# Transposing the activation rows of later chunks: a DRAM regroup plus VectorE transposes in place of DMA transposes, in a parallel attention and gated-MLP block

## The chip, the cores and the metric

The kernel runs on one core of one Trainium2 chip. The metric is the device time of one execution in microseconds (us). Three executions of the kernel before took 308.99, 309.40 and 310.95 us; their median, 309.4 us, is the time before. The profile comes from one more execution, of which the hardware recorded a span of 307.5 us from its first to its last instruction.

## What is computed

One layer whose attention and MLP branches read the same normalised rows and are added to the input. Shapes: x is 2048 rows by 640, 32 heads of 20, a sliding window of 256 keys, MLP width 1536, all in bfloat16.

```python
def reference(A_x, A_wqkv, A_wo, B_x, B_w_gate, B_w_up, B_w_down):
    xn = _layernorm(x)                               # over the 640 features
    q, k, v = split_heads(xn @ A_wqkv)               # 32 heads of 20
    s = (q @ k.T) * 20 ** -0.5                       # kept where 0 <= i - j < 256
    attn = (softmax(where(mask, s, -1e9)) @ v) @ A_wo
    mlp = (sigmoid(xn @ B_w_gate) * (xn @ B_w_up)) @ B_w_down
    return x + attn + mlp
```

Every matrix product with `xn` contracts over the 640 features, so TensorE needs the rows turned: features on the partitions, rows along the free dimension. How the rows of a chunk get turned is what the change is about.

## The kernel before

The 2048 rows are cut into four chunks of 512 rows (`c` = 0 to 3), each in four blocks of 128 rows (`s`). For each chunk there is one buffer `xnT[c]`, 128 partitions by 5 by 512: five slices `d`, each holding 128 of the 640 features for the 512 rows. Gate and up (`g_gu`, L407 to L423), the q and k projections (`proj_block`, L292) and v (`project_v`, L323) read it slice by slice and accumulate over the five slices.

**Input rows.** `xc[c]` holds the raw rows of a chunk. Its pool `xp` has a single buffer, so the load of the next chunk (`load_x`, L137) waits until every reader of the one before is done. Chunk 0 comes in four blocks over SyncE's queue (SP): L162 to L166, the first being all 128 rows of block 0.

**Chunk 0** is normalised block by block by VectorE (DVE) and ScalarE (ACT), and turned by TensorE (PE) against an identity matrix (`transpose_rows`, L276), five transposes a block.

**Chunks 1 to 3** are normalised by `g_norms` (L343): statistics per block, a pause of a few steps, then four times `norm_block` (L270, a DVE instruction that writes `xn`). Each `xn` is then turned by a DMA transpose on SP's queue, `turn_block` (L282): four per chunk, for chunk 3 in a generator of its own, `g_turns` (L361).

**Order.** Nothing is scheduled by a planner: the instructions of each engine stand in the order in which the code issues them. The attention runs over steps `t` (16 for chunk 0, 20 for each later one). A step issues a group of score matmuls into the single PSUM tile `ps` (L487), an exponential on ACT (L493) and two mask selects on GpSimd (L504) or a minimum on DVE (L497). Between steps, a list of filler parts (`Fill`) is pulled, each a generator that yields the PE time of what it has just issued. `mix(a, b, ...)` weaves a generator `b` into the steps of `a`. The parts around the change stand in this order (L689 to L707):

- `gu0a`, `gu0b`: gate and up of chunk 0, with the 11 or so steps of `norms1` woven in
- `x2`: the load of chunk 2's rows (L140), then `wo_i` (eight DRAM-to-DRAM DMAs, L212), `wd` (five DMAs, L205), `pads` (two DMAs that clear scratch, L178)
- `qk1`: the ten projection blocks of chunk 1. Each fills one of four PSUM tiles of `ps_d`; DVE (q, L301) or ACT (k, L303) copies it to `st`, a ring of six SBUF tiles (L118); SP stores `st` to a DRAM scratch (L305), from where `spread` (L315) brings heads back as `qT` and `kT`. After the fourth q block, `load_wo` (L217) issues four DMAs
- `v1`, `out0` (the down and output projections of chunk 0, with `norms2` woven in), `x3`, `qk2`, and so on

The same four PSUM tiles of `ps_d` serve the q, k, v, gate, up, down and output matmuls and the accumulators of the attention output (`acc`, L520). All SP work, loads, stores and transposes, stands in one queue and is issued in order; by the semaphores of the built program, each DMA also waits until the one eight places before it has landed.

`make_edge` (L238) fills a constant mask tile once: one memset and four selects, all on GpSimd, issued after the projections of chunk 0.

The weights are loaded with feature `c * 128 + p` on partition `p` of slice `c`:

```python
    wqkv_r = A_wqkv.rearrange("(c p) n -> p c n", p=P)
```

Of the kernel before, what the change touches and what calls it, by code (L numbers as in the profile page):

```python
# [9 lines left out]
P = 128  # L10
S = 2048
D = 640
# [3 lines left out]
DC = D // P  # L16
FC = F // P
CW = 512
NCH = S // CW
SBC = CW // P  # L20
# [6 lines left out]
FS = 768  # L27
# [9 lines left out]
BIG = 3.0e38  # L37
BF16 = mybir.dt.bfloat16
# [7 lines left out]
U = 64  # L46
# [47 lines left out]
def kernel(  # L94
# [11 lines left out]
    nc = tc.nc  # L106
    x2 = A_x.flatten_outer_dims()
    out2 = out.flatten_outer_dims()
    xr = x2.rearrange("(n p) d -> p n d", p=P)
# [25 lines left out]
    xc = {}  # L135

    def load_x(c):  # L137
        t = xp.tile([P, SBC, D], BF16, name="xc")
        xc[c] = t
        nc.sync.dma_start(out=t, in_=xr[:, c * SBC:(c + 1) * SBC, :])  # L140

    wqkv = [const.tile([P, DC, D], BF16, name="w" + part) for part in "qkv"]
    wqkv_r = A_wqkv.rearrange("(c p) n -> p c n", p=P)
    wg = [const.tile([P, DC, FS], BF16, name=f"wg{k}") for k in range(F // FS)]
    wu = [const.tile([P, DC, FS], BF16, name=f"wu{k}") for k in range(F // FS)]
    wd = const.tile([P, FC, D], BF16, name="wd")
# [5 lines left out]

    xc[0] = xp.tile([P, SBC, D], BF16, name="xc")

    def load_rows(s, queue):
        queue.dma_start(out=xc[0][:, s, :], in_=xr[:, s, :])  # L156

    def load_v(hf):
        a = hf * HALF
        nc.sync.dma_start(out=wqkv[2][:, :, a:a + HALF], in_=wqkv_r[:, :, 2 * D + a:2 * D + a + HALF])  # L160

    load_rows(0, nc.sync)  # L162
    load_rows(1, nc.sync)
    load_rows(3, nc.sync)
    load_v(0)
# [13 lines left out]

    def load_gu(t, w, k, lo=0, hi=FS):  # L180
        nc.sync.dma_start(out=t[k][:, :, lo:hi],
                          in_=w.rearrange("(c p) f -> p c f", p=P)[:, :, k * FS + lo:k * FS + hi])

    load_gu(wg, B_w_gate, 0, 0, FS // 2)
    load_gu(wu, B_w_up, 0, 0, FS // 2)
# [35 lines left out]
    ident = const.tile([P, P], BF16, name="ident")  # L221
# [14 lines left out]
    edge = const.tile([P, HG, 2 * U], BF16, name="edge")  # L236

    def make_edge():  # L238
        nc.gpsimd.memset(edge, BIG)
        for k, base, sign in ((0, -1, -1), (1, 0, 1)):  # L240
            for a in range(2):
                view = edge[a * U:(a + 1) * U, :, k * U:(k + 1) * U]
                nc.gpsimd.affine_select(out=view, in_=view, pattern=[[0, HG], [sign, U]],
                                        compare_op=GE, fill=0.0, base=base, channel_multiplier=-sign)

    xnT = {}
    xns = {}
# [13 lines left out]
    def ln_block(c, s, mv=None):  # L261
        return ln_mv(ln_half(c, s, 1, ln_half(c, s, 0)), mv)

    def rstd_blocks(mvs):
        rstds = lnp.tile([P, SBC], FP32, name="rstds", bufs=1)
        nc.gpsimd.tensor_scalar(out=rstds, in0=mvs[:, :, 1], scalar1=EPS, scalar2=None, op0=ADD)
        nc.gpsimd.tensor_tensor(out=rstds, in0=rstds, in1=neghalf, op=POW)
        return rstds

    def norm_block(c, s, mv, rstd):  # L270
        xn = lnp.tile([P, D], BF16, name="xn")
        nc.vector.tensor_scalar(out=xn, in0=xc[c][:, s, :], scalar1=mv[:, 0:1],  # L272
                                scalar2=rstd[:, 0:1], op0=SUB, op1=MULT)
        xns[c, s] = xn

    def transpose_rows(s, copy, lo=0, hi=DC):  # L276
        pt = ps_h.tile([P, DC, P], BF16, name="pt", tag="h")
        for d in range(lo, hi):
            nc.tensor.transpose(pt[:, d, :], xns[0, s][:, d * P:(d + 1) * P], ident)  # L279
        copy(out=xnT[0][:, lo:hi, s * P:(s + 1) * P], in_=pt[:, lo:hi, :])  # L280

    def turn_block(c, s):  # L282
        nc.sync.dma_start(out=xnT[c][:, :, s * P:(s + 1) * P], in_=xns.pop((c, s)), transpose=True)

    def new_xnT(c):
        xnT[c] = xtp.tile([P, DC, CW], BF16, name="xnT")
# [5 lines left out]
    def proj_block(w, c, m):  # L292

        ps = ps_d.tile([P, CW], FP32, name="pqk", tag="d")
        for d in range(DC):
            wt = wqkv["qk".index(w)][:, d, :].rearrange("p (k m) -> p m k", m=DC)
            nc.tensor.matmul(ps, lhsT=wt[:, m, :], rhs=xnT[c][:, d, :],  # L297
                             start=(d == 0), stop=(d == DC - 1))
        st = stp.tile([P, CW], BF16, name="st")
        if w == "q":  # L300
            nc.vector.tensor_copy(out=st, in_=ps)  # L301
        else:
            nc.scalar.copy(out=st, in_=ps)  # L303
        dst = scratch[w, c % 2].rearrange("(h j) s -> h j s", j=32)
        nc.sync.dma_start(out=dst[:, 4 * m:4 * m + 4, :], in_=st)  # L305
# [34 lines left out]

    MM = 216

    def g_norms(c, turn, gap=3):  # L343


        new_xnT(c)
        mvs = lnp.tile([P, SBC, nc.vector.BN_AGGR_DIM], FP32, name="mvs", bufs=1)
        for s in range(SBC):
            ln_block(c, s, mvs[:, s, :])
            if s == SBC - 1:  # L350
                rstds = rstd_blocks(mvs)
            yield 0
        for _ in range(gap):
            yield 0
        for s in range(SBC):
            norm_block(c, s, mvs[:, s, :], rstds[:, s:s + 1])
            yield 0
            if turn:
                turn_block(c, s)

    def g_turns(c):  # L361
        for s in range(SBC):
            turn_block(c, s)
            yield 0

    def g_qk(c):
        for w in "qk":
            for m in range(DC):
                proj_block(w, c, m)
                if c == 0 and w == "q" and m == 1:  # L370
                    load_x(1)
                if c == 0 and w == "q" and m == 3:
                    load_gu(wu, B_w_up, 0, FS // 2)
                if c == 1 and w == "q" and m == 3:
                    load_wo()
                if c and w == "k" and m == DC - 1:
                    spread("q", c, 0, GH)
                yield 5 * MM
        if c == 0:
            spread("q", c, 0, 2)  # L380
            spread("k", c, 0, 2)
            spread("q", c, 2, 4)
            spread("k", c, 2, 4)
# [19 lines left out]
    def part(w, d, f):  # L403
        k, first = divmod(f * P, FS)
        return w[k][:, d, first:first + P]

    def g_gu(c, f0, f1):  # L407
        for f in range(f0, f1):
            pg = ps_d.tile([P, CW], FP32, name="pg", tag="d")
            for d in range(DC):  # L410
                nc.tensor.matmul(pg, lhsT=part(wg, d, f), rhs=xnT[c][:, d, :],  # L411
                                 start=(d == 0), stop=(d == DC - 1))
            th = tp.tile([P, CW], FP32, name="th")
            nc.scalar.activation(out=th, in_=pg, func=TANH, scale=0.5)  # L414
            yield 5 * MM
            pu = ps_d.tile([P, CW], FP32, name="pu", tag="d")
            for d in range(DC):
                nc.tensor.matmul(pu, lhsT=part(wu, d, f), rhs=xnT[c][:, d, :],  # L418
                                 start=(d == 0), stop=(d == DC - 1))
            h = hp.tile([P, CW], BF16, name="h")  # L420
            ht[c, f] = h
            nc.vector.scalar_tensor_tensor(out=h, in0=th, scalar=1.0, in1=pu, op0=ADD, op1=MULT)  # L422
            yield 5 * MM  # L423
# [39 lines left out]
    def g_out(c, between, ahead=()):  # L463
        nxt = new_rows(c, 0)
        for s in range(SBC):
            rows = nxt
            if s == 0:
                yield from ahead
            if s + 1 < SBC:
                nxt = new_rows(c, s + 1)  # L470
            ys = [ps_d.tile([P, CW], FP32, name=f"y{i}", tag="d") for i in range(2)]
            for y, cut in zip(ys, HALVES):
                yield from down(c, s, y, cut)
            if s == 0:
                yield from between
            outp(c, s, ys, rows)
            yield 10 * 136
# [117 lines left out]
    def mix(a, b, first, every=1, rest=True):  # L595

        for k, cost in enumerate(a):
            yield cost
            if k >= first and (k - first) % every == 0:
                yield next(b, 0)  # L600
        if rest:
            yield from b
# [66 lines left out]
    nc.scalar.activation(out=scr, in_=neghalf[:, 0:1], func=EXP)  # L669
    banks.close()  # L670
    ps_s = banks.enter_context(tc.tile_pool(name="ps_s", bufs=1, space=bass.MemoryType.PSUM))
    for _ in g_qk(0):
        pass
    load_rest()
    make_edge()

    fill = Fill()
    GU = 10 * MM
    OUT = 4 * 34 * 136
    APART = 1800  # L680
    FIRST_PART = 1000
    def later(load, *args):
        load(*args)
        yield 0

    norms1 = g_norms(1, True)
    norms2 = g_norms(2, True)
    norms3 = g_norms(3, False, 6)
    fill.add("gu0a", mix(g_gu(0, 0, 4), norms1, 4, 1, False), 4 * GU)  # L689
    fill.add("gu0b", mix(g_gu(0, 4, 12), norms1, 0), 8 * GU)  # L690
    fill.add("x2", later(load_x, 2), 0)
# [7 lines left out]
    fill.add("qk2", g_qk(2), 50 * MM)  # L699
    fill.add("v2", mix(g_v(2), g_gu(1, 3, 7), 0, 1), 40 * 136 + 4 * GU)  # L700
    fill.add("gu1b", mix(g_gu(1, 7, 12), norms3, 0, 1, False), 5 * GU)
    fill.add("out1", mix(g_out(1, g_gu(2, 0, 1)), itertools.chain(norms3, g_turns(3)), 1, 2), OUT + GU)
    fill.add("qk3", g_qk(3), 50 * MM)
    fill.add("v3", mix(g_v(3), g_gu(2, 1, 5), 0, 1), 40 * 136 + 4 * GU)
    fill.add("gu2", g_gu(2, 5, 12), 7 * GU)
# [13 lines left out]
    for t, (c, k, o, step) in enumerate(todo):  # L719
# [11 lines left out]
        pt, late = scores(c, o, step)  # L731
# [12 lines left out]
    c = NCH - 1  # L744
# [6 lines left out]
    rows = [new_rows(c, s, *home, queue=nc.scalar) for s, home in enumerate(homes)]  # L751
# [55 lines left out]
```

## Time and profile before

| What | Value |
|---|---|
| Median of three executions | 309.4 us |
| Span of the profiled execution | 307.5 us |
| PE busy | 299.6 us (97%) |
| ACT busy | 198.4 us (65%) |
| DVE busy | 170.7 us (56%) |
| GpSimd (POOL) busy | 169.3 us (55%) |
| The 12 DMA transposes, each on SP's sequencer | 1.21 to 2.23 us |
| DMA moved | 35.68 MB, 116 GB/s on average |

In the profile, PE, DVE, ACT and POOL are the compute engines, PEld is TensorE's weight load and SPq is SyncE's queue. A line of a timeline gives the start in us from the start of the span, the duration, the engine, the source line, the operation, output<-input and how many instructions are merged. In the chain of waits the program is followed back from its last instruction, at each step to what released it. A DMA's line gives the time at which it is issued; its landing comes later and is read from the semaphore events of the trace. All line numbers named L are those of the kernel before.

### The profile page before, as it was taken

Reading aid. Unit: us, or ns where it says so; the run is one execution under the profiler, and the core shown is the slowest. Engines: PE = TensorE matmul, PEld = TensorE weight load, DVE = VectorE, ACT = ScalarE, POOL = GpSimd, SP = SyncE. Lnnn points to the kernel's source line nnn. Section 1 sums busy time; section 2 is a strip of 40 time slices with the busy share of each in tenths; the row PEclk is TensorE's granted clock in tenths of the full one; section 3 lists DMA queues with packets and bytes.
Section 4 is the critical chain, followed back from the end, with each engine's and each line's share of the span. In section 5 each row is a group of like instructions: output and inputs, shape, how many; then the busy total and the mean of one; then the engine's idle time right before and its main releaser. Section 6 shows DMA issues by size and latency. Waiting matters only on the chain.

```text
span 307.5 us, 9944 instructions
## 1 busy us (share of the span) xinstructions
PE 299.6 (97%) x4276; PEld 167.5 (54%) x4311; DVE 170.7 (56%) x339; ACT 198.4 (65%) x197; POOL 169.3 (55%) x308
## 2 busy tenths in 40 slices
PE   7999999999999999999999999999999999999995
PEld 3654444555657654554457654554546664444774
DVE  5633666639698364487946164392824536363523
ACT  6933877698855649888674547878585547687000
POOL 6000686787874828576683729467372937566000
PEclk9999999999999999999999999999999999999999
DMA  7997976986407352820002712730000200000202
GB/s 215 366 344 236 324 158 214 337 238 209 154 2 139 58 179 68 272 83 2 3 3 67 129 58 87 250 122 0 5 0 2 87 26 21 2 2 7 83 21 67
DMA packets 40460, 35.68 MB, mean 116 GB/s; under 512 B 10560, under 2 KB 39872, under 8 KB 40384
## 3 DMA queue, kind: packets, MB, share of 16 engines
q1 hardware_dynamic: 39552, 34.27, 37.3%
q10 hardware_dynamic: 864, 0.77, 0.9%
q8 instruction: 34, 0.56, 0.8%
q14 instruction: 10, 0.08, 0.1%
HBM read 23.63 MB, written 10.26 MB: 110 GB/s over the span
## 4 chain that ended last, share of the span: by engine, by line
PE 96%; issue 1%; DMA 1%; DVE 1%; ACT 0%; SPq 0%
PE y L432 18%; PE pu L418 17%; PE pg L411 17%; PE pqk L297 14%; PE ps L487 9%; PE pv L326 7%; PE y L439 7%; PE acc L520 6%; DMA xc<-in_A_x_dram 1%; PE pt L279 0%; ACT xn L617 0%; DVE xn L272 0%; DVE xn L628 0%; SPq L156 0%; DVE stats L252 0%
## 5 line engine op out<-in xcount | busy, mean ns | idle before, releaser
L504 POOL TENSOR_SCALAR_AFFINE_SELECT pT<-pT 64x512 bf16<-64x512 bf16 (+1 forms) x256 | 157.7, 616 | 108.1 <-ACT pT L493 95.6
L493 ACT ACTIVATE pT<-ps 128x2048 bf16<-128x2048 f32 (+1 forms) x76 | 141.0, 1855 | 59.6 <-PE ps L487 54.6
L422 DVE SCALAR_TENSOR_TENSOR h<-th,pu 128x512 bf16<-128x512 f32 x48 | 32.8, 684 | 52.6 <-PE pu L418 46.1
L418 PE MATMUL pu<-xnT,wu 128*128 128x512 bf16 x228 | 59.0, 380 | 0.7 <-issue 0.2
L411 PE MATMUL pg<-xnT,wg 128*128 128x512 bf16 x226 | 58.5, 380 | 0.9 <-issue 0.3
L432 PE MATMUL y<-wd,h 128*128 128x320 bf16 (+2 forms) x396 | 56.7, 295 | 0.0
L432 PEld LDWEIGHTS <-h 128*128 128x128 bf16 x396 | 36.7, 98 | 15.8 <-issue 2.0
L414 ACT ACTIVATE th<-pg 128x512 f32<-128x512 f32 x48 | 28.6, 595 | 15.5 <-PE pg L411 15.4
L411 PEld LDWEIGHTS <-wg 128*128 128x128 bf16 x240 | 22.2, 98 | 25.8 <-issue 1.8
L418 PEld LDWEIGHTS <-wu 128*128 128x128 bf16 x240 | 22.0, 98 | 25.5 <-issue 2.0
L487 PE MATMUL ps<-qT,kT 20*64 20x320 bf16 (+4 forms) x1440 | 32.1, 260 | 0.0
L532 DVE STREAM_TRANSPOSE t<-acc 128x512 f32<-128x512 f32 x32 | 21.1, 697 | 19.7 <-PE acc L520 19.7
L487 PEld LDWEIGHTS <-kT 20*64 20x64 bf16 x1440 | 15.4, 103 | 24.9 <-issue 21.8
L443 DVE SCALAR_TENSOR_TENSOR rows<-y,rows 128x320 bf16<-128x320 f32 x30 | 14.4, 488 | 25.5 <-PE y L439 25.3
L544 DVE TENSOR_TENSOR on<-t,rec 128x320 bf16<-128x320 f32 (+4 forms) x48 | 27.8, 580 | 1.1
L326 PE MATMUL pv<-wv,xnT 128*128 128x320 bf16 x160 | 25.7, 300 | 0.0
L439 PE MATMUL y<-wo,oc 128*128 128x320 bf16 (+2 forms) x165 | 24.2, 295 | 0.0
L297 PE MATMUL pqk<-xnT,wk 128*128 128x512 bf16 x97 | 23.1, 381 | 0.2
L297 PE MATMUL pqk<-xnT,wq 128*128 128x512 bf16 x94 | 22.8, 381 | 0.4 <-issue 0.2
L335 DVE CAST v<-pv 64x320 bf16<-64x320 f32 x29 | 14.1, 486 | 12.5 <-PE pv L326 12.3
L520 PE MATMUL acc<-pT,v 64*32 64x320 bf16 (+4 forms) x1440 | 19.7, 253 | 0.0
L520 PEld LDWEIGHTS <-v 64*32 64x32 bf16 x1440 | 16.2, 91 | 5.8 <-ACT pT L493 1.7
(50 smaller groups left out, 178.7 us busy)
## 6 DMA issues: line engine op xcount, KB each, us to landing
qT<-sq SPq DMA_DIRECT2D x16, 256.0 KB
kT<-sk SPq DMA_DIRECT2D x16, 256.0 KB
sq<-st SPq DMA_DIRECT2D x20, 128.0 KB
sk<-st SPq DMA_DIRECT2D x20, 128.0 KB
out_dram<-rows SPq DMA_DIRECT2D x15, 160.0 KB
wg<-in_B_w_gate_dram SPq DMA_DIRECT2D x4, 480.0 KB
wu<-in_B_w_up_dram SPq DMA_DIRECT2D x4, 480.0 KB
xc<-in_A_x_dram SPq DMA_DIRECT2D x3, 640.0 KB
```

The source lines that it names most:

```text
L297: nc.tensor.matmul(ps, lhsT=wt[:, m, :], rhs=xnT[c][:, d, :], start=(d == 0), stop=(d == DC - 1))
L326: nc.tensor.matmul(ps[:, 0:HALF], lhsT=xnT[c][:, d, s * P:(s + 1) * P], rhs=wqkv[2][:, d, hf * HALF:(hf + 1) * HALF], start=(d == 0), stop ...
L411: nc.tensor.matmul(pg, lhsT=part(wg, d, f), rhs=xnT[c][:, d, :], start=(d == 0), stop=(d == DC - 1))
L414: nc.scalar.activation(out=th, in_=pg, func=TANH, scale=0.5)
L418: nc.tensor.matmul(pu, lhsT=part(wu, d, f), rhs=xnT[c][:, d, :], start=(d == 0), stop=(d == DC - 1))
L422: nc.vector.scalar_tensor_tensor(out=h, in0=th, scalar=1.0, in1=pu, op0=ADD, op1=MULT)
L432: nc.tensor.matmul(y[:, 0:cut[1] - cut[0]], lhsT=ht[c, f][:, s * P:(s + 1) * P], rhs=wd[:, f, cut[0]:cut[1]], start=(f == 0), stop=False)
L439: nc.tensor.matmul(y[:, 0:cut[1] - cut[0]], lhsT=oc[c, m][:, s * P:(s + 1) * P], rhs=wo[:, m, cut[0]:cut[1]], start=False, stop=(m == DC - 1))
L487: nc.tensor.matmul(ps[a * U:(a + 1) * U, i, col * U:(col + n) * U], lhsT=qk["k", kc, o // GH][32 * i:32 * i + DH, o % GH + a, kb * U:(kb + ...
L493: nc.scalar.activation(out=pt[:, :, 0:width], in_=ps[:, :, 0:width], func=EXP, scale=SCALE)
L504: nc.gpsimd.affine_select(out=view, in_=view, pattern=[[0, HG], [0, n], [sign, U]], compare_op=GE, fill=0.0, base=base, channel_multiplier ...
L520: nc.tensor.matmul(acc[32 * i:32 * i + 32, q * U:(q + n) * U], lhsT=vt[kb][a * U:(a + 1) * U, u, h * VW:h * VW + 32], rhs=pt[a * U:(a + 1) ...
```

## The change

- The rows of chunks 1 to 3 are no longer turned by DMA transposes. Each normalised block is stored to a DRAM tile `xs` (`put_block`, four DMAs a chunk). Four more DMAs (`regroup`) read it back into `xc[c]`, over the raw rows, such that partition `32 b + j` holds, for each group of 32 rows, the 160 features of group `b` of row `j`. Five VectorE transposes (`turn`), which work in blocks of 32 by 32, then write the five slices of `xnT[c]`, reading every fifth element.
- By that, slice `d` holds the features `5 p + d`. The weights are loaded to match (`(p c)` in place of `(c p)`), and the transposes of chunk 0 read every fifth column.
- `g_norms` issues the four stores with the norms, then the regroup, then waits `lag` steps before the transposes, one a step. `g_turns` is gone; the calls get other gaps.
- Block 0 of chunk 0 is loaded in two halves of 64 rows, one from ACT's queue and one from SP's.
- `make_edge` is issued ahead of the projections of chunk 0, with its memset on VectorE.

```diff
-    wqkv_r = A_wqkv.rearrange("(c p) n -> p c n", p=P)
+    wqkv_r = A_wqkv.rearrange("(p c) n -> p c n", c=DC)
...
-    def load_rows(s, queue):
-        queue.dma_start(out=xc[0][:, s, :], in_=xr[:, s, :])
+    def load_rows(s, queue, a=0, b=P):
+        queue.dma_start(out=xc[0][a:b, s, :], in_=xr[a:b, s, :])
...
-    load_rows(0, nc.sync)
+    load_rows(0, nc.scalar, U, P)
+    load_rows(0, nc.sync, 0, U)
...
-                          in_=w.rearrange("(c p) f -> p c f", p=P)[:, :, k * FS + lo:k * FS + hi])
+                          in_=w.rearrange("(p c) f -> p c f", c=DC)[:, :, k * FS + lo:k * FS + hi])
...
-        nc.gpsimd.memset(edge, BIG)
+        nc.vector.memset(edge, BIG)
...
-            nc.tensor.transpose(pt[:, d, :], xns[0, s][:, d * P:(d + 1) * P], ident)
+            nc.tensor.transpose(pt[:, d, :], xns[0, s].rearrange("p (i d) -> p d i", d=DC)[:, d, :], ident)
...
-    def turn_block(c, s):
-        nc.sync.dma_start(out=xnT[c][:, :, s * P:(s + 1) * P], in_=xns.pop((c, s)), transpose=True)
+    xs = [tc.dram_tile([CW, D], BF16, name=f"xs{k}") for k in range(2)]
+
+    def put_block(c, s):
+        nc.sync.dma_start(out=xs[c % 2][s * P:(s + 1) * P, :], in_=xns.pop((c, s)))
+
+    def regroup(c):
+        rows = xs[c % 2].rearrange("(t j) (b f) -> b j t f", j=32, b=4)
+        for b in range(4):
+            nc.sync.dma_start(out=xc[c][32 * b:32 * b + 32].rearrange("j s (a f) -> j (s a) f", a=4), in_=rows[b])
+
+    def turn(c, d):
+        nc.vector.transpose(out=xnT[c][:, d, :], in_=xc[c].rearrange("p s (t d) -> p d (s t)", d=DC)[:, d, :])
...
-    def g_norms(c, turn, gap=3):
-        new_xnT(c)
+    def g_norms(c, gap=3, lag=3):
...
             norm_block(c, s, mvs[:, s, :], rstds[:, s:s + 1])
+            put_block(c, s)
             yield 0
-            if turn:
-                turn_block(c, s)
-
-    def g_turns(c):
-        for s in range(SBC):
-            turn_block(c, s)
+        regroup(c)
+        for _ in range(lag):
+            yield 0
+        new_xnT(c)
+        for d in range(DC):
+            turn(c, d)
             yield 0
...
+    make_edge()
     for _ in g_qk(0):
         pass
     load_rest()
-    make_edge()
...
-    norms1 = g_norms(1, True)
-    norms2 = g_norms(2, True)
-    norms3 = g_norms(3, False, 6)
+    norms1 = g_norms(1)
+    norms2 = g_norms(2)
+    norms3 = g_norms(3, 6, 2)
...
-    fill.add("out1", mix(g_out(1, g_gu(2, 0, 1)), itertools.chain(norms3, g_turns(3)), 1, 2), OUT + GU)
+    fill.add("out1", mix(g_out(1, g_gu(2, 0, 1)), norms3, 1, 2), OUT + GU)
```

## The prediction, made before the changed kernel ran

> **What bounds the kernel now.** I read the page's busy times, then its chain of waits by engine, then the timelines of SP, DVE, PE and ACT around the places where the change sits. The chain, by engine:
>
> ```profile
> PE 96%; issue 1%; DMA 1%; DVE 1%; ACT 0%; SPq 0%
> ```
>
> TensorE sets the time: 96% of the span is PE work standing end to end. No wait of PE for a DMA transpose appears anywhere in the table of waits, so taking the twelve transposes away can gain nothing by itself. The change can gain only at the start, and it can lose wherever it makes PE wait. So I looked for what PE could wait for in the new order, first for chunk 1, in SP's timeline:
>
> ```profile
> 39.32 5.27 SPq L283 DMA_TRANSPOSE xnT<-xn  x4
> 44.64 0.70 SPq L140 DMA_DIRECT2D xc<-in_A_x_dram  x1
> 45.40 5.04 SPq L212 DMA_DIRECT2D wo_i<-in_A_wo_dram  x8
> 50.48 4.34 SPq L205 DMA_DIRECT2D wd<-in_B_w_down_dram  x5
> 55.19 0.60 SPq L178 DMA_DIRECT2D sq<-kT  x1
> 56.15 0.56 SPq L178 DMA_DIRECT2D sk<-kT  x1
> 57.24 1.63 SPq L305 DMA_DIRECT2D sq<-st  x2
> ...
> 64.76 0.53 SPq L305 DMA_DIRECT2D sq<-st  x1
> ```
>
> Right behind the four transposes stand the load of chunk 2's rows, eight `wo_i`, five `wd` and two clears, and only then the stores of chunk 1's projections. SP is never idle here for long. What the reader should keep: the first `st` store is issued 12.6 us after the load at 44.64, and by the trace's landing events it lands at 64.55, 19.9 us after that load was issued. Most of this is DMA time, not SP time: the `wo_i` packets of 25,600 bytes take 0.95 us each, and on the slowest DMA engine the eight land one after the other from 50.12 to 57.09; `wd` follows there to 62.29, the clears to 64.21. Then ACT, DVE and PE in that stretch:
>
> ```profile
> 50.31 0.29 DVE L544 TENSOR_TENSOR on<-t,rec 128x128 bf16<-128x128 f32 x1
> 50.52 0.68 DVE L422 SCALAR_TENSOR_TENSOR h<-th,pu 128x512 bf16<-128x512 f32 x1
> 51.79 0.69 DVE L422 SCALAR_TENSOR_TENSOR h<-th,pu 128x512 bf16<-128x512 f32 x1 [0.59 <-PE pu L418]
> 54.57 0.69 DVE L422 SCALAR_TENSOR_TENSOR h<-th,pu 128x512 bf16<-128x512 f32 x1 [2.09 <-ACT th L414]
> ```
>
> ```profile
> 65.43 1.08 ACT L303 CAST st<-pqk 128x512 bf16<-128x512 f32 x2
> 66.37 1.92 ACT L493 ACTIVATE pT<-ps 128x2048 bf16<-128x2048 f32 x1
> ```
>
> ```profile
> 68.35 1.04 PE L520 MATMUL acc<-pT,v 64*32 64x320 bf16 x72
> 69.32 0.43 PE L487 MATMUL ps<-qT,kT 20*64 20x320 bf16 x24
> ```
>
> The ACT cast at 65.43 is the seventh `st` of the chunk. The ring has six, so it needs the first one's store to have landed: 64.55. It has 0.9 us to spare.
>
> **The change, part by part.** One price first. A turn is a 128x512 bf16 transpose on DVE; the nearest row is L548's, the same shape, 0.71 us, with contiguous input where the turn reads every fifth element. Below, the fastest DVE row of comparable bf16 size (L628, 128x640) is 0.45; above, I allow 1.4, twice L548. I take 0.71.
>
> *Chunk 1.* The norms end at 42.6. Four stores of 160 KB go out; such a store lands 1.8 us after issue when the queue is free (L454, issued 92.26, landed 94.06), so the last lands at 44.5. Four regroups at 0.45 us of issue each, the last issued about 46; a 256 KB read from DRAM lands 2.9 us after issue with little beside it (L315 at 123.20 and 123.72), so the data is there at 49. DVE is not at the turns before 50.6: its new order is the L544 above, turn 0, `h`, turns 1 and 2, `h`, turns 3 and 4, `h`. So: 50.6 + 0.71 + 0.69 + 1.42 + 0.69 + 1.42 = 55.5. PE wants slice 4 at 54.59 + 4 x 0.216 = 55.45, so the projections themselves hardly wait.
>
> The single `xc` buffer is what costs. It is now the source of the turns, so the load of chunk 2's rows waits for turn 4 instead of the last norm: 55.5 instead of 44.64, 10.9 us later. All that stands behind it on SP moves with it. I take the 19.9 us from load to first `st` landing as unchanged, since they are paced by the same packets and the same waits for the eighth DMA before: 55.5 + 19.9 = 75.4. ACT stands at the seventh `st` from 65.5 until then, in order, with the exponentials behind it. PE runs on until its next accumulator needs the PSUM tile that this cast frees, at 68.35, and stops. At 75.4 ACT does two casts (1.08), then the exponential of the scores of 65.71 (1.92): 78.4. The single `ps` tile holds PE's next scores until then. They stood at 69.32: **9.1 us lost**. By bounds: DVE's order and PE's pace put turn 4 no earlier than 53.8 (`h` after the up block that ends at 51.65, then two turns), 7.4 us lost; with turns of 1.4 us it is 59.0, 12.6 lost. The stores' second effect, on `kT` of chunk 1, moves by 8 to 9 us too and so adds nothing.
>
> PE has then stood for 7 us. How it restarts no row of mid-run shows; at the start of the span, ten 512-column matmuls (L232) stand 0.427 us apart against 0.216 later. So 0 to 2.1 us (10 x 0.211); I take 1.0, as part of that stretch waits for ACT anyway. [...]
>
> *Chunk 2.* The last norm ends at 98.15, its store lands at 100.0, the last regroup is issued at 101.4 and lands at 104.3. DVE stands there with turn 0 in front of the residual sums of block 2 (0.98) and four turns: 104.3 + 0.71 + 0.98 + 2.84 = 108.8. PE wants slice 4 at 107.38 + 0.86 = 108.25: 0.6 us, with the release of `y` tiles behind it 0.7; a free DVE would make it 0, turns of 1.4 us 3.5. The load of chunk 3 was issued after the last output store anyway (108.49), so it does not move.
>
> *Chunk 3.* Turn 4 stands behind the last residual sum, which ends at 178.56: 179.27 against 178.32 + 0.86. 0.1 us.
>
> *Start.* The first block lands at 3.07 and PE's first transposes start at 5.51. Halves may land up to 0.3 us sooner or no sooner. The transposes' weight loads now step over five elements: L297's `wq` loads, which do so too, take 119 ns against 98, and 20 of those make 0.4 us at most. I take 0, ends -0.3 and +0.4. [...]
>
> *At nothing:* the edge memset (0.69 us on POOL) falls into DVE's 0.66 us gap ahead of the first `st` at 14.18. The weights move in the same sizes and have slack (`wq` lands at 10.30, first used at 12.90). SP saves 12 x 1.23 us of transposes and gets 24 issues of about 0.45.
>
> Sum: 9.1 + 1.0 + 0.7 + 0.1 + 0 = 10.9 us. 307.5 + 10.9 = 318.4. The median lies 1.9 us above this profiled span, so 320.3, say **320**.
>
> **The rivals.** *The bulk loads' delay is hidden* (chance 0.13): the chain from load to first store shrinks when the queue has been empty for 6 us before it. It would have to shrink from 19.9 to 10.8 us. For it: DMA is busy only part of the time between 40 and 52 us. Against: eight `wo_i` packets of 0.95 us on one engine are 7.6, and `wd` and the clears another 6.7. Only the terms of chunks 2 and 3 would stay: 310.2.
>
> *The turns or the regroup are slow* (0.18): reads at every fifth element take 1.4 us, or 320-byte pieces into 32 partitions come 3 us later. Then chunk 1 loses 12.6 and chunk 2 up to 3.5: 307.5 + 17.2 + 1.9 = 326.6.
>
> *Faster* (0.07): the start is shortened and `xc` comes free early. It decides if the load of chunk 2's rows is issued by 46.4 (44.64 plus the 1.8 us between 10.9 and 9.1), so that PE never stops. The price then is the start alone: the chain's DMA share is 1%, a 2.3 us wait for x; were it halved, 308.2. Against: the last regroup cannot land before 47 even with free queues.
>
> **How the numbers follow.** My forecast has 0.62, around 320, its own range 316 to 323 by the bounds of the turn and the restart. The range reaches up to 327 for the slow turns and down to 310 for the hidden delay; outside lie about 0.12. About 1%, 3.1 us, is what can be told from no change here. Slower by over that: 0.62 + 0.18 and a little of the hidden case, 0.81; within: 0.15; faster: 0.04.
>
> **What would show it.** Right: PE idle for some 7 us around 69 to 78 us, ACT's cast of `st` waiting for a DMA there, SP's load of chunk 2's rows issued at about 55.5, five DVE transposes of about 0.7 us between 50 and 56, and the same pattern of at most 1 us at the heads of chunks 2 and 3. Wrong: PE without a gap at 70 us, that is, `st` stores landing in time although issued at 68; or DVE waiting in front of turn 0 for microseconds, which would put the cause in the regroup.

## The result, and the profile after

The changed kernel took 325.0 us (median of four executions, 323.06 to 325.66), the kernel before on the same chip 309.4 us (308.99 to 310.95). The ratio is 1.049, with a 95% interval of 1.045 to 1.053: slower by 5%. The profiled span went from 307.5 to 323.6 us. The forecast was 320 us with a range of 310 to 327; its own case was to lie between 316 and 323.

Line numbers from here on are those of each run's own kernel (the projections of L297 are L309 in the changed kernel, the turns L295). The page's chain of waits by engine, and its row of granted TensorE clock in 40 slices (9 is full):

```profile
PE 83%; DMA 8%; DVE 4%; SPq 2%; issue 1%; ACT 1%; DVEq 0%; ACTq 0%
PEclk9899999996899997999999999999999999999999
```

PE carried 96% of the chain before; now DMA, DVE and SP's queue hold 14% of it. And in three places the clock is below full.

To see where the 16 us lie, I followed single PE instructions through both traces: how much later does the same matmul start? The first v projections are 0.6 us late, the first q projection stands at 15.13 instead of 12.90 (+2.2), 0.3 more is lost on the way to the projections of chunk 1 (+2.5), behind those it is +11.7, at the head of chunk 2 it goes to +14.8 and a few us later to +16.4, and from there to the end nothing more is lost but 0.06. So there are three places: **start 2.2 us, chunk 1 9.2 us, chunk 2 4.8 us**.

**Start**, PE's timeline, first of the kernel before, then of the changed kernel, and of the latter one row of the table by windows (stretch, its length, busy us and counts of PE, PEld, DVE, ACT and POOL, then the granted clock, DMA share and GB/s):

```profile
5.51 0.45 PE L279 MATMUL pt<-ident,xn 128*128 128x128 bf16 x5 [0.69 <-DVE xn L272]
6.75 1.60 PE L326 MATMUL pv<-wv,xnT 128*128 128x320 bf16 x10
```

```profile
5.93 0.47 PE L280 MATMUL pt<-ident,xn 128*128 128x128 bf16 x5 [1.15 <-DVE xn L273]
7.38 2.69 PE L338 MATMUL pv<-wv,xnT 128*128 128x320 bf16 x10
7.60:10.90 3.30, 3.30 (x17) 2.06 (x16) 1.78 (x6) 3.08 (x9) 0.00 (x0) 0.50 1.00 314
```

The first transposes start 0.4 us late, and the ten matmuls of the first v projections run at half clock: the trace's record of the granted clock has 0.5 from 7.57 to 10.99.

**Chunk 1**, SP's timeline of the changed kernel:

```profile
41.54 3.65 SPq L286 DMA_DIRECT2D xs<-xn  x4
46.69 3.14 SPq L292 DMA_DIRECT2D xc<-xs  x4
57.18 0.40 SPq L140 DMA_DIRECT2D xc<-in_A_x_dram  x1
57.62 5.43 SPq L213 DMA_DIRECT2D wo_i<-in_A_wo_dram  x8
63.10 4.12 SPq L206 DMA_DIRECT2D wd<-in_B_w_down_dram  x5
...
69.45 3.90 SPq L317 DMA_DIRECT2D sq<-st  x4
```

SP issues the last regroup at 48.43 (this takes 1.39 us) and then stands still until 57.18. The load of chunk 2's rows (L140) was issued at 44.64 before. Its releaser is seen in DVE's timeline, where the fifth turn ends at 57.16:

```profile
52.62 0.75 DVE L295 STREAM_TRANSPOSE xnT<-xc 128x512 bf16<-128x512 bf16 x1
53.30 0.65 DVE L432 SCALAR_TENSOR_TENSOR h<-th,pu 128x512 bf16<-128x512 f32 x1
53.87 1.38 DVE L295 STREAM_TRANSPOSE xnT<-xc 128x512 bf16<-128x512 bf16 x2
55.17 0.65 DVE L432 SCALAR_TENSOR_TENSOR h<-th,pu 128x512 bf16<-128x512 f32 x1
55.74 1.42 DVE L295 STREAM_TRANSPOSE xnT<-xc 128x512 bf16<-128x512 bf16 x2
```

The turns themselves are quick and DVE does not wait for their data, though by a hair: the last regroup lands at 52.49, and turn 0 starts at 52.62. All that stands behind the load is late, and by the landing events the first `st` store lands at 76.61. Then ACT's and PE's timelines:

```profile
76.71 1.07 ACT L315 CAST st<-pqk 128x512 bf16<-128x512 f32 x2 [8.62 <-DMA sq<-st]
77.67 1.90 ACT L503 ACTIVATE pT<-ps 128x2048 bf16<-128x2048 f32 x1
```

```profile
77.35 2.27 PE L530 MATMUL acc<-pT,v 64*32 64x320 bf16 x72 [6.38 <-ACT st L315]
79.61 0.65 PE L497 MATMUL ps<-qT,kT 20*64 20x320 bf16 x24
```

ACT stood for 8.62 us at the seventh `st` of the chunk, PE for 6.38 us at the accumulators. Those 72 matmuls took 1.04 us before and 2.27 now: PE restarts at half clock. The table by windows shows it:

```profile
71.00:77.00 6.00, 0.00 (x0) 0.00 (x0) 0.00 (x0) 0.29 (x1) 0.00 (x0) 0.90 0.89 303
77.00:82.80 5.80, 5.42 (x107) 3.37 (x108) 2.35 (x5) 5.31 (x6) 2.67 (x5) 0.51 0.74 219
```

In the first row PE does nothing for 6 us while the DMA engines are 89% busy; in the second PE is busy at a clock of 0.51. Of the 9.2 us, 6.5 are the pause (the accumulators start at 77.35 instead of 68.35, less the 2.5 us from before) and 2.7 the half clock (5.42 us of work at 0.51 instead of 1.00 is 2.7).

**Chunk 2**, the timelines of SP, DVE and PE:

```profile
109.78 0.32 SPq L286 DMA_DIRECT2D xs<-xn  x1
110.15 0.42 SPq L459 DMA_DIRECT2D rows<-in_A_x_dram  x1
113.29 1.91 SPq L292 DMA_DIRECT2D xc<-xs  x4
```

```profile
118.91 0.75 DVE L295 STREAM_TRANSPOSE xnT<-xc 128x512 bf16<-128x512 bf16 x1 [6.09 <-DMA xc<-xs]
119.58 0.85 DVE L453 SCALAR_TENSOR_TENSOR rows<-y,rows 128x320 bf16<-128x320 f32 x2
120.36 2.63 DVE L295 STREAM_TRANSPOSE xnT<-xc 128x512 bf16<-128x512 bf16 x4
```

```profile
120.08 0.38 PE L309 MATMUL pqk<-xnT,wq 128*128 128x512 bf16 x1 [0.93 <-DVE rows L453]
121.14 0.38 PE L309 MATMUL pqk<-xnT,wq 128*128 128x512 bf16 x1 [0.67 <-DVE xnT L295]
```

The last normalised block ends at 109.74; the last regroup lands at 118.83, 9.1 us later. DVE stands at turn 0 for 6.09 us of that, with the residual sums (`rows`, L453) behind it, and PE waits first for these (they free the PSUM tile of `y`), then for one slice after the other. After that, 15 more projection matmuls of 512 columns take 5.04 us, against 3.43 before, and the clock is at half from 123.63 to 127.04. The lines are the changed kernel's, a row of its table by windows, and the kernel before's:

```profile
123.72 5.04 PE L309 MATMUL pqk<-xnT,wq 128*128 128x512 bf16 x15
123.70:127.00 3.30, 3.30 (x16) 1.19 (x9) 1.57 (x4) 1.88 (x1) 0.00 (x0) 0.50 0.35 84
```

```profile
107.38 1.24 PE L297 MATMUL pqk<-xnT,wq 128*128 128x512 bf16 x4
108.91 3.43 PE L297 MATMUL pqk<-xnT,wq 128*128 128x512 bf16 x15
```

### The profile page after: what moved, and what is told of

Its sections match the earlier page's. It is cut to its first block, busy times and chain, and to the rows that moved or that the text cites. A ratio compares the mean times of both kernels' runs of the same rounds, so it can differ in the third digit from the quotient of the medians.

```text
span 323.6 us, 10012 instructions
## 1 busy us (share of the span) xinstructions
PE 308.8 (95%) x4311; PEld 170.3 (53%) x4311; DVE 180.1 (56%) x355; ACT 198.5 (61%) x197; POOL 168.5 (52%) x307
## 4 chain that ended last, share of the span: by engine, by line
PE 83%; DMA 8%; DVE 4%; SPq 2%; issue 1%; ACT 1%; DVEq 0%; ACTq 0%
PE pu L428 16%; PE pg L421 15%; PE y L442 15%; PE pqk L309 11%; PE pv L338 8%; PE ps L497 7%; PE y L449 6%; PE acc L530 6%; DMA sq<-st 2%; DMA wo_i<-in_A_wo_dram 2%; DVE xnT L295 2%; SPq L213 1%; DMA xc<-xs 1%; DMA xs<-xn 1%; DMA xc<-in_A_x_dram 1%
## 5 line engine op out<-in xcount | busy, mean ns | idle before, releaser
L428 PE MATMUL pu<-xnT,wu 128*128 128x512 bf16 x240 | 59.8, 380 | 0.0
L421 PE MATMUL pg<-xnT,wg 128*128 128x512 bf16 x240 | 59.8, 380 | 0.0
L338 PE MATMUL pv<-wv,xnT 128*128 128x320 bf16 x160 | 28.3, 321 | 0.0
L309 PE MATMUL pqk<-xnT,wq 128*128 128x512 bf16 x100 | 25.6, 400 | 2.4 <-DVE xnT L295 1.4
L530 PE MATMUL acc<-pT,v 64*32 64x320 bf16 (+4 forms) x1440 | 20.9, 259 | 6.4 <-ACT st L315 6.4
L530 PEld LDWEIGHTS <-v 64*32 64x32 bf16 x1440 | 16.9, 93 | 12.7 <-ACT st L315 7.2
L309 PE MATMUL pqk<-xnT,wk 128*128 128x512 bf16 x100 | 23.2, 381 | 0.0
L453 DVE SCALAR_TENSOR_TENSOR rows<-y,rows 128x320 bf16<-128x320 f32 x30 | 14.1, 485 | 15.5 <-PE y L449 15.4
```

The source lines that it names most:

```text
L338: nc.tensor.matmul(ps[:, 0:HALF], lhsT=xnT[c][:, d, s * P:(s + 1) * P], rhs=wqkv[2][:, d, hf * HALF:(hf + 1) * HALF], start=(d == 0), stop ...
L530: nc.tensor.matmul(acc[32 * i:32 * i + 32, q * U:(q + n) * U], lhsT=vt[kb][a * U:(a + 1) * U, u, h * VW:h * VW + 32], rhs=pt[a * U:(a + 1) ...
```

## The experiments

My theory: chunk 1's loss comes from where the load of chunk 2's rows stands in SP's queue, chunk 2's from the round trip through DRAM, the start's from the first load in halves. For each there was a rival: that the loss of chunk 1 stays when the load moves, that DVE's own time makes chunk 2, and that the new weight layout makes the start. Each time below is a median of 4 to 10 executions, beside the kernel before, which took 309.1 to 309.3 us next to them; where a loss of a chunk or of the start is given, it is read from one profiled execution.

**1. The changed kernel with the first block loaded whole.**

```diff
-    load_rows(0, nc.scalar, U, P)
-    load_rows(0, nc.sync, 0, U)
+    load_rows(0, nc.sync)
```

> The changed kernel with one part undone: block 0 of chunk 0 is loaded whole from SP's queue again. Theory (the two queues issuing at once slow SP's first DMA issues, the first rows land 0.4 to 0.6 us late, and TensorE then runs the first v matmuls at half clock): the first q projection matmul stands near 13.1 us instead of 15.13, SP's first three x loads are issued by 2.2 us instead of 2.8, and the time is 325.0 - 2.0 = 323.0 us. Rival (the weights' new order of rows slows the loads of wv): the first q projection stays at 15.1 and the time at 325.

Measured: 322.2 us (321.47 to 324.64), ratio 1.043 [1.038, 1.047]. The first q projection stands at 13.21, 0.3 us behind that of before: of the start's 2.2 us, 1.9 are gone in this execution, in which the first v projections also run at full clock (1.60 us). The profiled execution (324.64) was the longest of the four; its chunks 1 and 2 lost 10.1 and 5.3 us, so it does not give the median's sum.

**2. The halves alone, in the kernel before.** The diff is the opposite of the one above, applied to the kernel before.

> The kernel before with one part of the change alone: block 0 of chunk 0 in two halves from two queues. Theory (halves slow the start): first q projection matmul at 14.5 to 15.1 us instead of 12.90, time 309.4 + 2.0 = 311.4 us. Rival (the weights' order or the strided transposes slow it): 309.4, within 0.3.

Measured: 311.2 us, ratio 1.0056 [1.0038, 1.0075]. The ten executions lie in two groups, two at 309.7 and 309.8 and eight from 311.0 to 311.9. The profile is of the lower group: its first q projection stands at 13.63, 0.7 us late, not the 2 us of the changed kernel. So the halves cost, but a profile of one execution does not show all of it. The record gives the mean granted clock of every execution: 1.00 in the two short ones, 0.993 or 0.994 in six of the eight long ones, 1.00 in the other two (311.0 and 311.1). An execution with one stretch of 3.41 us at half clock has 0.994 (run 8's profile). So half clock goes with six of the eight; for the other two the record does not tell (last section).

**3. The new weight layout alone, in the kernel before.** The weights are loaded as `(p c)` and chunk 0's transposes read every fifth column. The rows of chunks 1 to 3 are still turned by DMA, in another order of features than the weights, so the output is not the reference's.

```diff
-    wqkv_r = A_wqkv.rearrange("(c p) n -> p c n", p=P)
+    wqkv_r = A_wqkv.rearrange("(p c) n -> p c n", c=DC)
...
-            nc.tensor.transpose(pt[:, d, :], xns[0, s][:, d * P:(d + 1) * P], ident)
+            nc.tensor.transpose(pt[:, d, :], xns[0, s].rearrange("p (i d) -> p d i", d=DC)[:, d, :], ident)
```

> The kernel before with the weights in the new order of rows and chunk 0's transposes reading every fifth column; the rows of chunks 1 to 3 are still turned by DMA transposes, so they stand in another order of features than the weights and their outputs are not the reference's, while every instruction and its size stay. Theory (halves are to blame for the start): 309.4 to 309.8 us, first q projection matmul at 12.9 to 13.3. Rival (the layout is to blame): 311.4, first q projection at 15.

Measured: 309.7 us, ratio 1.0007 [0.9988, 1.0026]. The first q projection is 0.4 us late (13.34) and the last matmul of the kernel 0.36: small, and the rival for the start falls.

**4. The changed kernel with the load of chunk 2's rows behind `v1`.** The suspected wait alone is moved; the turns, the DRAM round trip and the halves stay.

```diff
-    fill.add("x2", later(load_x, 2), 0)
     fill.add("wo_i", later(turn_wo), 0)
...
     fill.add("v1", mix(g_v(1), g_gu(1, 0, 2), 1, 2), 40 * 136 + 2 * GU)
+    fill.add("x2", later(load_x, 2), 0)
```

> The changed kernel with the load of chunk 2's rows moved on SP's queue: behind the projections of chunk 1 and their stores instead of in front of wo_i, wd and the clears. It still waits for the fifth turn, but nothing that PE needs stands behind it. Theory (the wait itself is harmless, the queue behind it costs 9.2 us in chunk 1): no gap of PE at 71 to 77 us, no ACT cast that waits for a store for more than 1 us, time 325.0 - 9.2 = 315.8 us (315 to 317). Rival (the DRAM regroup and the turns themselves, or the weaker DMA start, cost the time): 324 to 325.

Measured: 313.9 us, ratio 1.015 [1.011, 1.019]; chunk 1 loses 0.4 us in place of 9.2. SP issues `wo_i` at 48.80 and the load at 77.72, and PE's timeline has no gap:

```profile
69.60 1.04 PE L530 MATMUL acc<-pT,v 64*32 64x320 bf16 x72
70.85 0.43 PE L497 MATMUL ps<-qT,kT 20*64 20x320 bf16 x24 [0.21 <-ACT pT L503]
```

One line of order gives 11.1 us back, more than the 9.2 that I expected, because in the profiled execution the start lost 1.0 instead of 2.2 us and chunk 2 only its wait of 3.0: it kept full clock at both places (mean clock 1.00). That the load's place caused chunk 1's loss is shown.

**5. The changed kernel with nine `st` buffers instead of six.** If ACT's wait is for a free `st`, three more must move it by three casts.

```diff
-    stp = pool("stp", 6)
+    stp = pool("stp", 9)
```

> The changed kernel with nine st tiles instead of six. Theory (ACT stands at the cast that needs a ring tile whose store has not landed): the cast that waits is now the tenth, not the seventh, still until the first store lands at 76.6; PE gets through the accumulators and one score group before it stops, so chunk 1 loses 4.5 us instead of 9.2: 325.0 - 4.7 = 320.3 us (319 to 322). Rival (PE waits for the q and k that come back from DRAM, whatever the ring): 325.

Measured: 322.3 us, ratio 1.042 [1.036, 1.047]. ACT's and PE's timelines:

```profile
77.43 0.59 ACT L315 CAST st<-pqk 128x512 bf16<-128x512 f32 x1 [6.74 <-DMA sq<-st]
```

```profile
79.85 0.55 PE L497 MATMUL ps<-qT,kT 20*64 20x320 bf16 x16 [5.65 <-ACT pT L503]
80.33 2.85 PE L338 MATMUL pv<-wv,xnT 128*128 128x320 bf16 x10
```

It is now the tenth cast that waits, as it must be if the ring is the gate. But the gain I expected was more than what came: the stores land when they land, PE still pauses for 5.65 us, and 5.2 us of half clock follow (ten `pv` matmuls in 2.85 us instead of 1.53). Chunk 1 loses 8.2 instead of 9.2, and I had expected 4.5. The rest of the 2.7 us between the medians lies elsewhere: in the profiled execution chunk 2 lost 2.2, with full clock behind its waits (15 projection matmuls in 3.43 us). Three more buffers did not make up for a queue that is 10 us late.

**6. Run 4 without the DRAM round trip.** The stores and the regroup are left out; the turns read the raw rows, so chunks 1 to 3 are computed from unnormalised, unregrouped rows and the output is not the reference's. DVE's work stays.

```diff
-            put_block(c, s)
...
-        regroup(c)
```

> The kernel of e4 (load of chunk 2's rows behind the projections of chunk 1) without the stores of the normalised rows to DRAM and without the regroup: the turns read the raw rows of the chunk as they are, so the outputs are not the reference's, while the fifteen turns stay. Theory (chunk 2 loses 3.0 us because DVE waits for the regroup): DVE reaches the turns 6 us sooner and the loss falls to 0 to 0.3; with chunk 1's 0.4 gone too, 313.9 - 3.3 = 310.6 us (310.2 to 311.5). Rival (the turns' own DVE time, 0.65 us each in front of the first projection): 313 to 314.

Measured: 311.2 us, ratio 1.0066 [1.0042, 1.0089]. DVE's timeline at the head of chunk 2:

```profile
102.51 0.75 DVE L295 STREAM_TRANSPOSE xnT<-xc 128x512 bf16<-128x512 bf16 x1
103.19 0.85 DVE L451 SCALAR_TENSOR_TENSOR rows<-y,rows 128x320 bf16<-128x320 f32 x2
103.96 2.67 DVE L295 STREAM_TRANSPOSE xnT<-xc 128x512 bf16<-128x512 bf16 x4
```

With the same DVE instructions in the same order and no wait, chunk 2 loses 0.0 us. So its loss is the wait for the round trip, with the half clock that may follow it; DVE's time is free there.

**7. What is left when all three are mended.** Run 4 with the first block whole and `norms2 = g_norms(2, 1, 5)`: the norms of chunk 2 closer together, the turns two steps later.

> The changed kernel with three parts altered: block 0 loaded whole, the load of chunk 2's rows behind the projections of chunk 1 on SP, and the norms of chunk 2 two steps earlier (a pause of 1 instead of 3, then 5 steps instead of 3 before the turns). Theory (the three losses are the start's two queues, SP's order in chunk 1, and the round trip through DRAM that ends after chunk 2's first projection is due): start +0.35, chunk 1 +0.4, chunk 2 1.3 instead of 3.0 as the last norm moves 1.7 us ahead, in all 309.3 + 2.1 = 311.4 us (310.5 to 312). Rival (chunk 2's loss is the DVE time of the turns, not the wait for the regroup): chunk 2 stays at 3.0, 313.

Measured: 312.1 us, ratio 1.009 [1.006, 1.013]. Chunk 2 still loses 1.1 us, since DVE stands at turn 0 for 5.22 us (the round trip takes long here too), 0.5 us go near the norms of chunk 2, 0.4 at chunk 1 and 0.6 at the start. No version that I ran beats the kernel before.

**8. The halves again, in the kernel before, but both from SP's queue.** I had blamed the two queues.

```diff
-    load_rows(0, nc.sync)
+    load_rows(0, nc.sync, U, P)
+    load_rows(0, nc.sync, 0, U)
```

> The kernel before with block 0 in two halves, both from SP's queue. Theory (ACT and SP issuing at the same moment make SP's first two issues 0.6 and 0.8 us instead of 0.4): SP issues five DMAs at 0.4 to 0.45 us each, block 0 lands at about 3.5, the rows after it 0.45 us later than before; first q projection matmul at 13.2 to 13.4, 309.7 us. Rival (the split into halves itself costs): as with two queues, 311.2 us and 13.6 to 15.

Measured: 311.5 us (309.9 to 311.73), ratio 1.0063 [1.0041, 1.0086]. My theory of two colliding queues fell: one queue is no better. A load of 128 rows took 0.39 us to issue before; the two loads of 64 rows take 0.60 and 0.58. By the landing events the first block is there at 3.90 (3.07 before, 3.46 in the changed kernel with its two queues) and the second at 4.72 (before 3.55). PE's timeline:

```profile
6.50 0.45 PE L280 MATMUL pt<-ident,xn 128*128 128x128 bf16 x5 [2.02 <-DVE xn L273]
...
8.14 2.62 PE L327 MATMUL pv<-wv,xnT 128*128 128x320 bf16 x10
```

The first transposes are 1.0 us late, and the ten `pv` matmuls that took 1.60 us before take 2.62, nearly as in the changed kernel (2.69). Here the clock record has 0.5 from 6.95 to 10.36. Of the five executions, the short one (309.9) has a mean clock of 1.00, three of the four long ones 0.994.

**9 to 11. Two more warm-up matmuls**, so that PE idles less between the warm-up and the first transposes: in run 2's kernel (9), in the kernel before (10) and in the changed kernel (11).

```diff
-    for n in (6, 4):
+    for n in (6, 6):
```

> Before, with only the first block of x loaded in halves from two queues, and two warm-up matmuls more (twelve, so that PE is busy until about 5.7 us and idle only 0.3 us ahead of the first transposes at 5.96). Theory (the halves cost 0.7 us by their later landing in every execution, and some 1.5 us more in those executions in which the longer idle time sends PE to half clock): the first v projection takes 1.60 us, the first q projection stands at 13.6, the median is 309.9 (309.5 to 310.3) and no execution lies near 311.3. Rival (the later arrival of what stands behind the halves costs it, and the clock has no part): 311.2 again.

> The kernel before with two warm-up matmuls more (twelve), nothing else. PE is busy to about 5.26 us instead of 4.83, the first transposes at 5.51 don't wait. Theory: no change of the typical execution, 309.3 (308.9 to 309.7), but none near 311. Rival (the warm-up itself shifts the start, or saves clock in the kernel before too): 308.5 or 310.5.

> The changed kernel with two warm-up matmuls more (twelve). Theory (of the start's 2.2 us, some 1.3 to 1.5 are half clock after the idle time behind the warm-up): the first v projection takes 1.60 instead of 2.69 us, the first q projection stands at 13.6 to 13.9 instead of 15.13, the median is 323.6 (322.8 to 324.2). Rival (the start's loss is late data only): 15.1 and 325.0 again. The stops at chunks 1 and 2 stay under both.

Measured: run 9 took 310.2 us, ratio 1.0040 [1.0023, 1.0057]; eight of its ten executions lie from 309.6 to 310.4 and two at 311.7 and 312.0, where without the two matmuls eight of ten were at 311 and more. Run 10 took 309.5 us, 1.0008 [0.9994, 1.0021]: no change. Run 11 took 323.5 us, 1.047 [1.045, 1.050], 1.5 less than the changed kernel, but the two intervals overlap; its first q projection stands at 14.11 instead of 15.13. PE's timeline of run 9:

```profile
6.30 0.45 PE L280 MATMUL pt<-ident,xn 128*128 128x128 bf16 x5 [0.18 <-DVE xn L273]
...
7.72 1.60 PE L327 MATMUL pv<-wv,xnT 128*128 128x320 bf16 x10
```

The data come no sooner, yet `pv` runs at full clock. It did so in run 2's profile too, so the profiles do not set runs 2 and 9 apart; the executions do. A mean clock of 0.994 or less stands beside six of ten in run 2 and beside one of ten in run 9 (the one at 311.7). So the two matmuls make half clock at the start rarer, without excluding it, and my forecast that no execution would lie near 311.3 was wrong.

Run 11 does not show by its profile that a shorter pause did it: ahead of the first transposes PE waits 1.38 us there, against 1.15 in the changed kernel, and yet the clock stays full (mean clock 0.984 against 0.979, one step of half clock fewer). Nor need the 1.0 us by which its q projection stands earlier come from the warm-up, for run 4 has the changed kernel's start unaltered, kept full clock in its profile, and has its first q projection at 13.93.

So the start's 2.2 us are two things. Run 4 gives the later data alone: 1.0 us, of which 0.7 are the halves (run 2) and the rest is near what the new layout costs (0.3 in run 1, 0.4 in run 3). The remaining 1.2 are half clock.

## Why the prediction was right, and where its steps were off

**The bulk delay at chunk 1** (9.1 us to the scores): right in mechanism and close in size. Taken without the 2.5 us that came from ahead of it, the load was issued at 54.7 (forecast 55.5), and from there the first `st` landed 19.4 us later (forecast 19.9). Both were slightly shorter, so the scores came 7.8 us late instead of 9.1. Every station, the cast, the exponential, the accumulators, is in the trace as forecast, and run 4 shows that the load's place alone makes it.

**The restart** (1.0, ends 0 and 2.1): 1.4 us were lost behind the scores, the rest of the half clock being covered by ACT's exponential, which ended at 79.57 as the scores started at 79.61. The forecast took its ends from the spacing of the first matmuls of the span, and the 1.0 between them was my own estimate. Behind the pause of 6.4 us the granted clock was 0.51 (77.00 to 82.80); it came back 5.3 us after the restart here and 5.2 in run 5. In the clock record it falls at 75.84 and rises at 82.67, two steps of 3.41 us, and PE was busy for 1.9 us of the first step and for all of the second. Half clock also followed steps in which PE was not wholly idle (last section).

**Chunk 2** (0.7): the wrong term. The step that failed is "its store lands at 100.0, the last regroup is issued at 101.4 and lands at 104.3", that is, 6.2 us from the norm to the data. It took 9.1: the store 3.4 instead of 1.8 (issued 109.78, landed 113.22), the last regroup 4.1 instead of 2.9 (issued 114.72). With 2.9 us more, the forecast's own sum of 0.6 becomes 3.5, against 3.2 measured; and 1.6 us of half clock came on top, for which the forecast had no term at chunk 2. Run 6 shows that the round trip is the cause.

Both prices were those of a DMA alone. The first of the four regroups did land 2.9 us after its issue (113.29, 116.15); the others are issued 0.4 to 0.5 us apart but land 0.8 to 1.0 apart, which I read as the last one being late by what those ahead of it still have to move. The rival "slow regroup" named 3 us for this; 1.2 came from there and 1.6 from the store. Its other half, slow turns, was not there: a turn took 0.72 to 0.76 us against my 0.71.

The store's 3.4 us are one late part. It lands in sixteen parts: fifteen are there 1.79 us after the issue, the last 1.65 us after those. Meanwhile, from 110.71 to 112.02, the trace has a packet of 16,384 bytes of the kind that the page calls `instruction`. The kernel before had such cases: of its fifteen stores of L454 eleven took 1.8 to 2.1 us, and each of the four that took 2.3 to 3.9 has such a packet beside it (issued 108.10, fifteen parts after 1.87 us, the last after 3.43; packet from 109.14 to 110.41). The forecast took its 1.8 from the common rows. In chunk 1 the store issued at 44.87 took 1.76, in run 4 the last store of chunk 2 took 3.2, again with such a packet. That the packet holds up the one part is argued from the times, since the trace does not tell which DMA engine moved it.

**Chunk 3** (0.1): 0.06.

**Start** (0, ends −0.3 and +0.4): the second wrong term, outside its ends by 1.8 us. The step that failed is "halves may land up to 0.3 us sooner or no sooner": the DMAs of 64 rows cost 0.6 us of issue each, and the block landed 0.4 us later, the next one 0.6. The other failure is a term that was missing: the forecast priced a slower restart behind the stop at chunk 1 and did not ask what a longer gap between the warm-up and the first transposes does to the clock; that was 1.2 us. Runs 2 and 8, 311.2 us with two queues and 311.5 with one, show the halves alone as a loss, of which 0.7 us came from later data alone in run 2's profile.

**At nothing**: the memset did not stop PE, and the saved DMA transposes won nothing, as no one had waited for them. The weights, put at nothing for their slack, were not quite free: by run 3 the new layout costs 0.4 us at the start, where the second half of `wv` lands 0.8 us later and PE waits for it.

The two wrong terms together make 6.3 us, chunk 1 gives back 0.9 of its 10.1, and 0.3 were lost ahead of it: 10.9 + 6.3 − 0.9 + 0.3 = 16.6 us, against 16.5 measured at the last matmul; the span grew by 16.1. The sign was right because the largest term was. That the range held is in part luck: 325.0 lies above the forecast's own 316 to 323, and the range reached to 327 only for slow turns, which did not come; what lifted the time there are the two wrong terms. Of the rivals, the hidden bulk delay and the faster start did not happen.

Two sums of the forecast were a little off. With turns of 1.4 us, chunk 2 by its own formula comes to 104.3 + 1.4 + 0.98 + 5.6 = 112.3, a loss of 4.0 and not 3.5, and the rival to 327.1. And `wd` with the clears, 57.09 to 64.21, is 7.1 us and not 6.7. Neither changes the argument.

## What to carry to other kernels

When a buffer gets a second reader, look at who reuses it, and at all that stands in order behind that one DMA on its queue: here a buffer freed 10 us later held up loads and stores that had nothing to do with it, and moving one line gave most of it back. Price a round trip through DRAM from rows that have the same neighbours in the queue, not from a DMA alone, and from the slow rows as well as the common ones. And a pause of TensorE can cost more than its own length: here 6.5 us of pause brought 2.7 of half clock, and at the start 1.0 us of late data brought 1.2. Whether it does so can differ between executions of one kernel, so look at the clock of all of them and not at one profile.

## What the runs showed of the hardware

- In the changed kernel's trace the record of the granted clock begins at 4.16 us, with full clock, and changes at 7.57, 10.99, 75.84, 82.67, 123.63 and 127.04: always after whole steps of 3.41 us (3.413 by the longest stretch, 197.97 us for 58 of them). The steps fall at other times in each execution: the first entry stands at 3.54 us in run 8, 4.24 before, 6.29 in run 9 and 9.92 in run 5, while the first matmul starts at 0.83 or 0.84 in each. The warm-up matmuls agree: in the changed kernel they start 0.43 us apart up to 3.77 and the last two, behind 4.16, 0.22 apart; ten of them take 3.64 us in run 8 and 4.43 in run 5, and the twelve of run 9 take 5.28, which is 0.43 apart to the end. Before its first entry the record has nothing: in run 5 the first ten `pv` matmuls take 2.66 us instead of 1.60 and the start is 1.9 us late, but the mean clock of 0.989 is no lower than the two steps at chunk 1 alone make it.
- A step need not be wholly idle for half clock to follow. It followed steps in which PE was busy for 1.60 us (start of the changed kernel, 4.16 to 7.57), for 1.39 (start of run 8) and for 1.97 (chunk 2 of the changed kernel, 120.21 to 123.63). It did not follow the changed kernel's step from 69.01 to 72.42, with 1.95. And nearly the same waits of PE at chunk 2, 0.7 to 0.9 us and four of 0.26 to 0.67, brought half clock in the changed kernel (15 matmuls in 5.04 us) and not in run 4 (14 in 3.19). So these runs give no threshold.
- A weight load in the new layout takes 0.62 and 0.56 us of SP's time to issue (`wv`, in the changed kernel; 0.66 and 0.56 in run 3) instead of 0.43, and the second half of `wv` lands at 8.85 instead of 8.07 (run 3), at the same size.
